# Two small strided reads of the weights at the head of ScalarE's queue, with memsets and filling products in other places

## The chip, the cores and the metric

One core of a Trainium2 chip runs the kernel. The metric is the device time of one execution in microseconds (us), on one core; lower is better. Engines are named as the profile names them: PE (TensorE products), PEld (TensorE weight loads), DVE (VectorE), ACT (ScalarE), POOL (GpSimd), SP (SyncE). SPq and ACTq are the DMA issues of SP and ACT.

## The reference

One transformer block with modulation (adaLN), 2048 tokens of 448 features, bf16:

```python
mod = (_silu(c) @ w_mod).reshape(c.shape[0], 6, 1, -1)
sa, ca, ga, sb, cb, gb = (mod[:, 0].copy(), ..., mod[:, 5].copy())
h = _layernorm(x, axis=-1) * (1 + ca) + sa
x = x + ga * _A_ref(h, A_wqkv, A_wo)
h = _layernorm(x, axis=-1) * (1 + cb) + sb
x = x + gb * _B_ref(h, B_w_in, B_w_sp, B_b_sp, B_w_out)
```

`_A_ref` is attention with 16 heads of 28, in which a token sees itself and the 255 before it. `_B_ref` is a gated MLP: gelu(x @ w_in) is split in two halves of 896, the second is normalised and mixed over all tokens by w_sp (2048 x 2048), multiplied with the first and projected by w_out. w_mod is 448 x 2688, w_qkv 448 x 1344.

## The kernel before

The tokens are 16 tiles of 128; features lie in four chunks of 128 (448 is padded to 512). The program has five streams, one for each engine. The order in each is written out by hand in the table ORDER: a word is the number of an operation in order of definition, the letter of its engine (p, a, v, g, s for PE, ACT, DVE, POOL, SP) and, for some, a slot. Waits on semaphores are derived from the dependencies that each operation names, so each engine works through its list in order, and an operation that waits holds up all behind it.

The stages are: loads, modulation and QKV of tiles 0 to 3 (to some 20 us); attention with the QKV of the other tiles beside it (to some 110 us); the MLP's first product (to some 155 us); mixing over tokens (to some 245 us); projection and output.

The opening, which the change touches, runs so. SP issues the loads one after another: x for tiles 0, 1 (`d_x00`) and 2, 3 (`d_x01`), four chunks of 960 columns of w_mod (`t_wmA`), three chunks of w_qkv's Q and K columns (`t_wq`), the V columns, x for tiles 4 to 7, the rest of w_mod (`t_wmB`), and more. ACT issues c and the last 64 rows of w_qkv (`d_wq3`). DVE clears paddings and takes statistics of x tiles (L580, L583); POOL turns these into rs_all by an addition (L585) and a power (L586); DVE writes the normalised tile xn (L593). TensorE transposes c by products with a one (L520), ACT takes Silu of it into sc_sb (L524, L525), and TensorE multiplies sc_sb with the four chunks of w_mod (L537, one group of eight products for a chunk), which DVE sums into modT (L542). TensorE transposes xn (L624), four tiles in two pairs; each feature chunk is scaled by modT into hT (L634 on ACT, L635 on DVE). Weights for Q and K are spread to 32 columns for a head in WQK (L572, L573), and L644 multiplies WQK and hT: 32 products of 512 columns. Between these stand products of a tile wz of zeros into an unused bank (`warm`, L550), fillers that keep TensorE at work and that nothing reads. L557 is the second use of w_mod, by `t_wmB`; L712 transposes tiles 4 to 7, and L722 scales them into hT. L840 is the exponential of attention.

The fillers' definition, and the group on the fourth w_mod chunk, are

```python
    def warm(n, dur, times, cols):
        for _ in range(n):
            hW = Hold(bH)
            hW.until.append(pe(dur, [lambda e, hW=hW: e.matmul(
```

```python
            [t_wmA[kc], t_sc, t_p2] + t_mA[-1:], -60.0 + 0.1 * kc, [] if kc else [hA]))
```

Of the kernel before, what the change touches and what calls it, by code (L numbers as in the profile page):

```python
# [19 lines left out]
57.v 0.a 3.a 26.v 1.s 2.s 4.s 34.g 23.v 24.v 27.v 43.a 5.s 35.g 6.s 36.g 58.p.0 59.p.0 60.p.0 44.p.0 7.s 139.v 40.g 50.a 32.g 8.s 137.v 37.g 140.v 9.s  # L20
25.v 138.v 143.v 141.g 38.g 10.s 145.v 142.g 146.v 28.v 144.v 45.a 11.s 46.a 147.g 149.v.0 148.g 151.v.1 12.s 61.p.0 62.p.0 63.p.0 64.p.0 65.p.0
66.p.0 67.p.0 68.p.0 69.p.0 70.p.0 150.p.2.3 152.p 13.s 153.v.2 52.p.1 53.p 71.p.0 54.p 155.v.3 14.s 55.p 154.p 29.v 156.p 15.s 16.s 56.v 133.a 157.v
21.s 134.v 158.a 159.v 72.p.0 73.p.0 74.p.0 191.p.4 17.s 171.p.5 135.g 186.p.6 160.v 18.s 161.p.0 136.a 172.p 162.p 192.p 49.g 176.p.1 163.p 47.a
177.p 196.p.2 166.p.3 42.g 193.p 41.g 164.p 213.v 167.p 165.a 173.p 178.p 215.v 168.p 48.a 174.p 51.v 179.p 214.v 217.v 197.p 169.p 175.a 219.v 187.p
198.p 170.a 199.p 39.v 181.p.0 180.a 188.p 218.v 220.v 194.p 216.v 200.v 189.p 221.g 195.a 182.p 222.g 183.p 30.v 184.p 190.a 374.p.0 185.v 205.p.1
375.a.0 229.g 225.g 211.s 227.g 223.g 122.p.0 228.v.0 226.g.1 212.s 201.p.6 224.v.2 19.s 230.g.3 123.v 206.a 380.p.0 125.s 202.v 231.p.0 381.a.1 210.s
234.p.1 232.v 124.s 235.v 399.p.0 233.a 203.p.6 209.s 236.v 400.a.2 269.v 251.p.0 31.v 271.v 401.a 243.p.1 376.v 265.v 126.s 252.a 406.p.0 267.v 127.s
407.a.3 241.p.0 244.v 270.v 266.v 268.v 239.p.1 272.v 204.v 408.a 273.g 274.g 242.v 377.p.0 240.a 402.v 426.p.0 378.v 237.p.0 279.g 427.a.4.0 382.v
277.g 319.v 33.g 428.p.0 281.g 280.v.0 379.p 263.p.1 275.g 320.v 282.v.1 285.s 276.g.2 321.v 238.a 434.p.0 384.v 278.g.3 247.p.0 264.v 435.a.5.1 283.s
409.v 383.p 129.g 249.p.1 248.v 284.s 322.v 411.v 385.p 429.a 455.p.0 131.g 250.v 245.p.0 456.a.6.2 386.v 323.v 286.s 132.g 387.v.0 207.p.1 325.v  # L30
403.p.0 256.s 457.p.0 246.v 208.a 463.p.0 458.a 253.s 404.v 259.p.1 464.a.0.3 438.v 255.s 439.v 405.p 410.p 388.s 261.p.0 430.v 431.v 412.p 262.a
484.p.0 254.s 413.v 287.v 436.p.0 485.a.1.4 414.v.1 257.p.0 459.v 432.p.0 288.v 433.p 290.v 440.p 258.v 437.a 492.p.0 289.v 260.a 465.p.0 489.v 441.p
493.a.2.0 295.p.0 326.v 460.v 442.v 305.p.1 488.v 466.a 324.v 443.v.2 327.g 513.p.0 296.a 328.g 468.v 444.s 515.p.0 514.a.3.1 461.p.0 467.v 462.p
291.p.0 335.g 497.v 415.s 130.g 306.v 469.p 516.a 521.p.0 292.v 329.g 470.p 522.a.4.2 331.g 336.v.0 297.p.1 333.g 332.v.1 330.g.2 471.v 472.v.0
486.p.0 445.p.0 496.v 473.s 487.a 542.p.0 298.a 446.v 494.p.0 543.a.5.3 490.p.0 447.v 22.s 389.p.1 334.v.3 337.s 526.v 491.p 303.p.0 390.v 495.a 517.v
338.s 550.p.0 304.a 525.v 301.p.1 551.a.6.4 546.v 339.s 391.v 293.p.0 518.v 498.p 302.a 340.s 554.v 552.p.0 499.p 294.a 571.p.0 500.v 553.a 501.v.2
474.p.1 310.s 572.a.0.0 307.s 299.p.0 475.v 309.s 476.v 523.p.0 519.p.0 502.s 524.a 555.v 520.p 300.a 579.p.0 448.v 547.v 317.p.1 580.a.1.1 341.g
308.s 477.v 527.p 576.v 528.p 311.p.0 478.g 342.v 479.g 392.v 318.a 529.v 344.v 573.p.0 530.v.1 480.g 600.p.0 574.a 343.g 312.v 416.p.1 531.s
601.a.2.2 449.g 584.v 544.p.0 503.p.0 450.g 417.v 20.s 393.g 575.v 548.p.0 545.a 608.p.0 504.v 549.p 418.v 556.p 609.a.3.3 505.v 315.p.1 419.v 420.g
# [24 lines left out]
1052.a 1051.p 994.g 941.v 1031.v 1072.p.2 1054.a 987.g 880.s 1010.v 898.v 1055.a 915.g 1081.p.3 995.v 1003.v 1011.g 970.v 876.s 1073.p.1 1012.g 959.v
1024.v 1082.p 1004.g 988.v 884.s 1005.g 1013.v 1083.p 1006.v 1074.p 916.v 1086.a 887.s 1075.p 1087.a 1076.a 1100.p.6 1077.a 873.s 1078.a 1079.a 1085.a
# [201 lines left out]
def bass_adaLN_cond__sliding_block__mixer_gmlp__prompt_kernel(  # L267
# [924 lines left out]
```

## Time and profile before

| What | us |
|---|---|
| median of three executions (lowest, highest) | 277.14 (276.2, 277.36) |
| the profiled execution, its whole time | 277.13 |
| its span in the profile | 275.4 |
| PE busy in the span | 265.9 (97%) |
| DVE busy | 162.9 (59%) |
| ACT busy | 128.2 (47%) |
| POOL busy | 111.6 (41%) |

The granted TensorE clock is 1.00 throughout. The page gives the busy share of each engine in 40 slices of 6.9 us, in tenths:

```profile
PE   8898999998999999999999999999999999999995
DVE  7578999997899899696799202110340300341543
ACT  3598899997999999847756500000000000000000
DMA  7995362457344777949699999000000000001123
```

In the stretch from 20 to 110 us, three engines are nearly full; from 155 us on TensorE alone is. A row of the time line has the start, the length from the first instruction's start to the last one's end, engine, line, operation, output and inputs, the number of instructions, and in brackets the idle time of the engine before it with what ended it. A row of the chain of waits has start, length, and what the chain ran through.

### The profile page before, as it was taken

What the parts mean: (1) busy time and instruction counts of PE and PEld (TensorE: products, weight loads), DVE (VectorE), ACT (ScalarE), POOL (GpSimd) and SP (SyncE); (2) the same over time, 40 slices, a digit from 0 to 9 for tenths busy, and PEclk for the clock granted to TensorE, in tenths of its full rate; (3) what the DMA queues carried; (4) which work ended last, traced back from release to release, by engine and by line L of the source; (5) the groups of instructions that cost most, each with busy time, mean ns of one, the idle gap of its engine ahead of it and who ended that gap; (6) DMA issues with size and microseconds to landing.
All of it is one profiled execution on the core that took longest, in us unless ns stands there. A gap on an engine that the chain in (4) does not pass through costs nothing.

```text
span 275.4 us, 7324 instructions
## 1 busy us (share of the span) xinstructions
PE 265.9 (97%) x3174; PEld 139.3 (51%) x3196; DVE 162.9 (59%) x365; ACT 128.2 (47%) x152; POOL 111.6 (41%) x185
## 2 busy tenths in 40 slices
PE   8898999998999999999999999999999999999995
PEld 2544566465667575544444444444444444454452
DVE  7578999997899899696799202110340300341543
ACT  3598899997999999847756500000000000000000
POOL 4440914126644714864549103140361730370400
PEclk9999999999999999999999999999999999999999
DMA  7995362457344777949699999000000000001123
GB/s 207 339 253 147 88 88 33 93 96 204 82 71 71 98 116 153 144 100 167 110 184 175 172 190 187 0 2 0 0 1 2 0 0 0 2 0 33 60 67 109
DMA packets 66862, 26.48 MB, mean 96 GB/s; under 512 B 57801, under 2 KB 65742, under 8 KB 66830
## 3 DMA queue, kind: packets, MB, share of 16 engines
q1 hardware_dynamic: 66748, 25.90, 46.1%
q8 instruction: 25, 0.41, 0.6%
q10 hardware_dynamic: 82, 0.12, 0.1%
q14 instruction: 7, 0.06, 0.1%
HBM read 9.47 MB, written 1.84 MB: 41 GB/s over the span
## 4 chain that ended last, share of the span: by engine, by line
PE 73%; DVE 11%; DMA 7%; ACT 4%; SPq 2%; POOL 1%; issue 1%
PE ps L1077 35%; PE ps L1032 8%; PE ps L1053 8%; PE ps L1094 7%; DMA hT<-o_sb 4%; ACT PW L840 4%; PE ps L947 4%; PE ps L922 3%; PE ps L879 3%; DVE st_all L580 3%; DMA x_sb<-in_A_x_dram 3%; DVE PT L895 2%; PE ps L777 1%; PE ps L764 1%; PE ps L735 1%
## 5 line engine op out<-in xcount | busy, mean ns | idle before, releaser
L840 ACT ACTIVATE PW<-ps 128x2048 bf16<-128x2048 f32 (+1 forms) x56 | 67.1, 1244 | 4.5 <-PE ps L879 1.8
L1081 DVE TENSOR_TENSOR tmpg<-ps,bsp_bc 128x512 bf16<-128x512 f32 x28 | 19.0, 689 | 74.6 <-PE ps L1077 64.6
L1084 POOL TENSOR_TENSOR z1T<-tmpg,z1T 128x512 bf16<-128x512 bf16 x28 | 31.7, 1151 | 73.7 <-DVE tmpg L1081 73.6
L1077 PE MATMUL ps<-wspB,z 128*128 128x512 bf16 x219 | 49.2, 379 | 0.3
L1077 PE MATMUL ps<-wspA,z 128*128 128x512 bf16 x219 | 48.7, 379 | 0.4 <-issue 0.2
L895 DVE TENSOR_TENSOR PT<-PW,mask 128x1024 bf16<-128x1024 bf16 x56 | 36.3, 673 | 0.7 <-ACT PW L840 0.7
L1077 PEld LDWEIGHTS ps<-wspA,z 128*128 128x128 bf16 x224 | 21.8, 98 | 26.6 <-DVE z L1044 0.4
L1077 PEld LDWEIGHTS ps<-wspB,z 128*128 128x128 bf16 x224 | 21.9, 98 | 26.3
L585 POOL TENSOR_SCALAR ve_all<-mv_all 128x1 f32<-128x1 f32 (+2 forms) x37 | 10.1, 280 | 48.3 <-DVE mv_all L583 47.8
L586 POOL TENSOR_TENSOR rs_all<-ve_all,neghalf 128x1 f32<-128x1 f32 (+2 forms) x37 | 26.2, 717 | 1.0
L922 PE MATMUL ps<-Vaug,PT 128*128 128x29 bf16 x496 | 24.8, 176 | 0.0
L922 PEld LDWEIGHTS ps<-Vaug,PT 128*128 128x128 bf16 x496 | 22.3, 96 | 4.4 <-DVE o_sb L938 0.9
L1032 PE MATMUL ps<-w_in,hT 64*128 64x448 bf16 x224 | 22.9, 349 | 0.0
L1053 PE MATMUL ps<-hT,w_in 64*128 64x512 bf16 x196 | 22.5, 376 | 0.0
L1094 PE MATMUL ps<-w_out_g,z1T 128*128 128x448 bf16 x105 | 20.7, 352 | 0.0
L922 PE MATMUL ps<-Vaug,PW 128*128 128x29 bf16 x224 | 20.4, 175 | 0.0
L580 DVE BATCH_NORM_STATS2 st_all<-x_sb 128x6 f32<-128x448 bf16 x32 | 18.9, 613 | 1.5 <-DMA x_sb<-in_A_x_dram 1.4
L580 DVE BATCH_NORM_STATS2 st_all<-z 128x6 f32<-128x448 bf16 x32 | 18.5, 605 | 2.1 <-ACT z L1039 2.0
L735 PE MATMUL ps<-hT,WQK 128*128 128x512 bf16 x69 | 17.8, 380 | 1.4 <-issue 0.3
L922 PEld LDWEIGHTS ps<-Vaug,PW 128*128 128x128 bf16 x224 | 17.7, 96 | 2.2
L1061 ACT ACTIVATE z1T<-ps 128x512 bf16<-128x512 f32 x28 | 14.8, 610 | 7.1 <-PE ps L1053 7.0
L1039 ACT ACTIVATE z<-ps 128x896 bf16<-128x896 f32 x16 | 14.1, 914 | 6.8 <-PE ps L1032 6.8
(112 smaller groups left out, 326.6 us busy)
## 6 DMA issues: line engine op xcount, KB each, us to landing
out_dram<-fin SPq DMA_DIRECT2D x15, 112.0 KB, 1.7
x_sb<-in_A_x_dram SPq DMA_DIRECT2D x3, 448.0 KB, 7.0
w_in<-in_B_w_in_dram SPq DMA_DIRECT2D x1, 1344.0 KB, 6.3
wmod<-in_w_mod_dram SPq DMA_DIRECT2D x1, 1296.0 KB, 10.8
QBD<-qT SPq DMA_DIRECT2D x16, 64.0 KB, 2.9
w_out_g<-in_B_w_out_dram SPq DMA_DIRECT2D x1, 784.0 KB, 5.8
wmod<-in_w_mod_dram SPq DMA_DIRECT2D x3, 240.0 KB, 5.6
wq_st<-in_A_wqkv_dram SPq DMA_DIRECT2D x3, 224.0 KB, 5.8
```

The costliest lines, as they stand in the source:

```text
L580: st = [dve(0.62 if True else 0, lambda e, t=t, ci=ci, s=s: e.bn_stats(st_all[:, slot, t, ci, :], s()), deps(t), prio) for ci, s in enumer ...
L586: rs = pool(0.53 + 0.15 * len(tiles), lambda e: e.tensor_tensor(rs_all[:, slot, a:b], ve_all[:, slot, a:b], neghalf[:, 0:b - a], ALU.pow), ...
L735: m = pe(4 * MMS, [lambda e, h=h, g=g, kc=kc, tb=tb: e.matmul(ps[:, h.slot[0], :], lhsT=WQK[:, kc, 4 * g:4 * g + 4, :].rearrange("p a b -> ...
L840: ex = act(xdur, lambda e, out_ap=out_ap, in_ap=in_ap: e.activation(out_ap(), in_ap(), ACT.Exp, scale=SCALE), [s], v - 8.0 + u, takes, tab ...
L895: return dve(0.70, lambda e: e.tensor_tensor(cols(hp.slot[0] * 2048 + 1024 * k, [[256, 4], [128, 2], [1, 128]]), cols(at_w() + 128 + 192 * ...
L922: fns.append(lambda e, hp=hp, hO=hO, hi=hi, bi=bi, kb=kb, hd=hd, nb=nb, a=at[hi][bi], p_of=p_of: e.matmul(ps[:, hO.slot[0], 32 * hd:32 * h ...
L1032: return lambda e, kc, p0, start, stop: e.matmul(ps[:, hs[t % 2].slot[hf], 0:D], lhsT=hT[p0:p0 + 64, kc, t * 128:(t + 1) * 128], rhs=w_in[ ...
L1053: return lambda e, kc, p0, start, stop: e.matmul(ps[:, hs[b // 2].slot[b % 2], :], lhsT=w_in[p0:p0 + 64, kc, ft * 128:(ft + 1) * 128], rhs ...
L1077: m = pe(16 * MMS, [lambda e, h=h, si=si, ft=ft, tb=tb: e.matmul(ps[:, h.slot[0], :], lhsT=z2[:, si, ft * 128:(ft + 1) * 128], rhs=(wspA i ...
L1081: a = dve(0.7, lambda e, h=h, ht=ht, tb=tb: e.tensor_tensor(tmpg[:, ht.slot[0], :], ps[:, h.slot[0], :], bsp_bc[:, tb * 512:(tb + 1) * 512 ...
L1084: u = pool(1.16, lambda e, ht=ht, ft=ft, tb=tb: e.tensor_tensor(z1T[tb][:, ft, :], tmpg[:, ht.slot[0], :], z1T[tb][:, ft, :], ALU.mult), [ ...
L1094: return [lambda e, ft=ft: e.matmul(ps[:, h.slot[0], 0:D], lhsT=z1T[t // 4][:, ft, (t % 4) * 128:(t % 4 + 1) * 128], rhs=w_out_g[:, ft, :] ...
```

## The change

Six edits, all within the first 10 us of the program:

1. Two loads are added on ACT's queue, into a new tile `early`: 64 rows of w_mod, every seventh, and 32 rows of w_qkv, every fourteenth, 32 columns (64 bytes) of each. The first stands ahead of the load of c, the second between c and `d_wq3`. Nothing reads `early`; the products on the fourth w_mod chunk wait for both loads.
2. On TensorE two fillers move from behind the transposes of c (L520) to ahead of them.
3. On TensorE two more fillers stand between the products on the fourth w_mod chunk and the second pair of transposes.
4. On DVE the memsets of zero, one, sc_sb and sc_sb's single element move ahead of or between the two memsets of wmod.
5. On POOL the first rs_all moves ahead of the memset of WQK's padding.
6. All operation numbers from 4 on rise by two, since two operations are new; this is most of the table's difference.

```diff
+    early, _, _ = alloc("early", [64, 2, 32], BF16)
...
     t_wq3 = load("d_wq3", "act", 0.23, lambda e: e.dma_start(wq_st[0:64, 3, 0:2 * D], A_wqkv[384:448, 0:2 * D]), prio=-98.97, land=5.5)
+    t_early = [load("d_e0", "act", 0.01, lambda e: e.dma_start(early[:, 0, :], w_mod[0:448:7, 0:32]), prio=-98.999, land=3.5),
+               load("d_e1", "act", 0.01, lambda e: e.dma_start(early[0:32, 1, :], A_wqkv[0:448:14, 0:32]), prio=-98.99, land=4.0)]
...
-            [t_wmA[kc], t_sc, t_p2] + t_mA[-1:], -60.0 + 0.1 * kc, [] if kc else [hA]))
+            [t_wmA[kc], t_sc, t_p2] + t_mA[-1:] + (t_early if kc == 3 else []), -60.0 + 0.1 * kc, [] if kc else [hA]))
...
-57.v 0.a 3.a 26.v 1.s 2.s 4.s 34.g 23.v 24.v 27.v 43.a 5.s 35.g 6.s 36.g 58.p.0 59.p.0 60.p.0 44.p.0 7.s 139.v 40.g 50.a 32.g 8.s 137.v 37.g 140.v 9.s
+59.v 4.a 0.a 5.a 3.a 25.v 26.v 27.v 28.v 1.s 2.s 6.s 36.g 30.v 29.v 45.a 7.s 37.g 8.s 38.g 60.p.0 61.p.0 62.p.0 63.p.0 64.p.0 46.p.0 9.s 141.v 42.g
```

The table moves instructions; these are the places. On ACT, the start of its list, before:

```order
L420 DMA c_row<-in_c_dram 1x448
L425 DMA wq_st<-in_A_wqkv_dram 64x896
L518 ACT_TABLE_LOAD
L518 ACTIVATE zero<-zero 128x1 [waits dve]
L529 ACTIVATE QBD<-zero 128x1024
L524 ACTIVATE sc_sb<-ps 128x3 [waits pe,dve]
```

and now (lines are three to seven higher there):

```order
L427 DMA early<-in_w_mod_dram 64x32
L421 DMA c_row<-in_c_dram 1x448
L428 DMA early<-in_A_wqkv_dram 32x32
L426 DMA wq_st<-in_A_wqkv_dram 64x896
L521 ACT_TABLE_LOAD
```

The load of c is second and that of the last w_qkv rows fourth in the queue.

On TensorE, the products on w_mod and the second transposes, before:

```order
L550 MATMUL ps<-wz 128x512
L537 MATMUL ps<-sc_sb,wmod 128x1 [waits d_wmA2]
L537 MATMUL ps<-sc_sb,wmod 128x1 x7
L537 MATMUL ps<-sc_sb,wmod 128x1 [waits d_wmA3]
L537 MATMUL ps<-sc_sb,wmod 128x1 x7
L624 MATMUL ps<-ident,xn 128x128 [waits dve]
```

and now:

```order
L540 MATMUL ps<-sc_sb,wmod 128x1 [waits d_wmA2]
L540 MATMUL ps<-sc_sb,wmod 128x1 x7
L540 MATMUL ps<-sc_sb,wmod 128x1 [waits d_e0,d_e1,d_wmA3]
L540 MATMUL ps<-sc_sb,wmod 128x1 x7
L553 MATMUL ps<-wz 128x512 x2
L627 MATMUL ps<-ident,xn 128x128 [waits dve]
```

Two products of wz stand ahead of the transposes, and the last group waits for the two new loads too.

On POOL, the first statistics, before:

```order
L585 TENSOR_SCALAR ve_all<-mv_all 128x2 [waits dve]
L506 MEMSET WQK 128x128x4
L586 TENSOR_TENSOR rs_all<-ve_all,neghalf 128x2 [waits pool]
L585 TENSOR_SCALAR ve_all<-mv_all 128x2 [waits dve]
L586 TENSOR_TENSOR rs_all<-ve_all,neghalf 128x2 [waits pool]
```

and now:

```order
L588 TENSOR_SCALAR ve_all<-mv_all 128x2 [waits dve]
L589 TENSOR_TENSOR rs_all<-ve_all,neghalf 128x2 [waits pool]
L509 MEMSET WQK 128x128x4
L588 TENSOR_SCALAR ve_all<-mv_all 128x2 [waits dve]
L589 TENSOR_TENSOR rs_all<-ve_all,neghalf 128x2 [waits pool]
```

The memset went from ahead of the first rs_all to behind it.

More of the change, by code (lines that the diff above doesn't have):

```diff
@@ L24 @@
[L24 to L39, printed above, removed]
@@ new lines @@
+249.p.0 266.v 437.a.5.1 285.s 411.v 385.p 131.g 251.p.1 250.v 286.s 324.v 413.v 387.p 431.a 457.p.0 133.g 252.v 247.p.0 458.a.6.2 388.v 325.v 288.s
+134.g 389.v.0 209.p.1 327.v 405.p.0 258.s 459.p.0 248.v 210.a 465.p.0 460.a 255.s 406.v 261.p.1 466.a.0.3 440.v 257.s 441.v 407.p 412.p 390.s 263.p.0
+432.v 433.v 414.p 264.a 486.p.0 256.s 415.v 289.v 438.p.0 487.a.1.4 416.v.1 259.p.0 461.v 434.p.0 290.v 435.p 292.v 442.p 260.v 439.a 494.p.0 291.v
+262.a 467.p.0 491.v 443.p 495.a.2.0 297.p.0 328.v 462.v 444.v 307.p.1 490.v 468.a 326.v 445.v.2 329.g 515.p.0 298.a 330.g 470.v 446.s 517.p.0
@@ new lines @@
+516.a.3.1 463.p.0 469.v 464.p 293.p.0 337.g 499.v 417.s 132.g 308.v 471.p 518.a 523.p.0 294.v 331.g 472.p 524.a.4.2 333.g 338.v.0 299.p.1 335.g
+334.v.1 332.g.2 473.v 474.v.0 488.p.0 447.p.0 498.v 475.s 489.a 544.p.0 300.a 448.v 496.p.0 545.a.5.3 492.p.0 449.v 24.s 391.p.1 336.v.3 339.s 528.v
+493.p 305.p.0 392.v 497.a 519.v 340.s 552.p.0 306.a 527.v 303.p.1 553.a.6.4 548.v 341.s 393.v 295.p.0 520.v 500.p 304.a 342.s 556.v 554.p.0 501.p
+296.a 573.p.0 502.v 555.a 503.v.2 476.p.1 312.s 574.a.0.0 309.s 301.p.0 477.v 311.s 478.v 525.p.0 521.p.0 504.s 526.a 557.v 522.p 302.a 581.p.0 450.v
@@ new lines @@
+456.s 614.v 612.p.0 349.p.0 590.v.2 354.a 644.v 660.p.0 613.a 591.s 608.p.0 350.v 661.a.6.1 563.p.1 615.v 130.s 662.p.0 399.v 643.v 609.p 400.s 616.p
+425.g.0 564.v 663.a 668.p.0 484.v 617.p 664.v 669.a.0.2 315.p.0 357.s 636.v 485.s 633.p.0 565.v 534.p.1 618.v 566.v 316.a 619.v.1 567.g 689.p.0
+512.g.1 634.a 535.v 359.p.0 690.a.1.3 426.g 665.v 427.s 637.p.0 673.v 638.p 641.p.0 360.v 645.p 358.s 642.a 536.v 697.p.0 620.s 646.p 694.v 698.a.2.4
+691.p.0 363.p.1 537.v 647.v 693.v 356.s 538.g 672.v 592.p.0 355.s 364.a 568.g 648.v.0 718.p.0 692.a 513.g 593.v 649.s 569.g 367.p.1 841.g 719.a.3.0
@@ new lines @@
+702.v 666.p.0 670.p.0 514.s 368.v 667.p 674.p 671.a 594.v 726.p.0 723.v 675.p 727.a.4.1 621.p.0 701.v 595.v 699.p.0 596.g 622.v 373.p.1 843.g 866.s
+676.v 700.a 677.v.2 570.g.2 747.p.0 374.v 361.p.0 748.a.5.2 539.g 678.s 623.v 540.g 695.p.0 597.g 722.v 696.p 703.p 598.g 858.s 541.v.0 720.p.0 362.a
+599.g.1 755.p.0 721.a 731.v 704.p 756.a.6.3 650.p.1 542.g 705.v 543.s 706.v.1 749.p.0 365.p.0 651.v 624.v 752.v 750.a 776.p.0 707.s 625.g 751.v
+724.p.0 777.a.0.4 679.p.1 626.g 730.v 627.g 728.p.0 600.v 680.v 725.p 601.s 732.p 759.v 729.a 784.p.0 366.a 571.v 760.v 757.p.0 572.s 733.p 758.a
@@ new lines @@
+928.p 901.a 654.g 655.g 929.p 630.s 656.g 908.p.0 715.g.1 937.a 1034.p.1 685.g 716.v 896.v 770.g 930.a 839.g 717.s 909.p.2 657.v.2 910.p 658.v 938.v
+659.s 795.p.0 686.v.0 912.a 687.g 835.g 824.p.1 796.v 688.s 903.v 911.p 771.g 825.v 944.p.0 772.g 919.a 913.v 836.g 863.s 945.p.3 740.v 914.v 741.g
+773.v.1 946.p 797.v 860.s 947.p 849.v 948.a 774.v 798.v 1042.p.2 850.v 799.g 826.v 857.s 955.a 742.g 950.v 1043.p.0 775.s 743.g 852.g 827.v 931.v
+1044.p 744.v.2 800.g 851.v 1035.p.3 921.v 1047.a 828.g 829.g 1046.a 745.v 957.v 1036.p 746.s 830.g 915.v 902.v 801.g 1037.p 1039.a 831.v.0 1045.p
@@ new lines @@
+832.v 802.v.1 1040.a 833.s 920.v 803.g 962.p.2 1038.a 956.v 1041.a 963.p.1 932.v 1049.a 804.s 1048.a 933.v 964.p 904.v 958.v 895.v 905.g 934.g 980.p.3
+966.a 965.p 871.s 1058.p.0 973.a 981.p.2 853.a 862.s 855.g 974.v 982.p 935.g 1059.p.1 854.g 867.s 984.a 906.g 983.p 986.v 856.g 1060.p 868.s 991.a
+949.v 1061.p 975.v 1063.a 967.v 1066.p.3 865.s 1062.a 993.v 1064.a 1016.p.2 936.v 1065.a 968.v 859.s 1017.p.0 992.v 897.v 1018.p 994.v 976.v 922.v
+985.v 861.s 977.g 1019.p 923.g 978.g 1020.a 998.p.1 898.g 1027.a 1022.v 872.s 1067.p.2 1021.v 951.v 1068.p 1028.v 952.g 864.s 916.g 939.v 899.g
@@ new lines @@
+999.p.0 1071.a 924.g 1023.v 940.v 979.v 1070.a 1069.p 959.g 925.v 870.s 1000.p 995.g 969.v 1029.v 1073.a 970.g 953.g 1001.p 907.v 1002.a 941.g
+1050.p.3 1024.g 942.g 1009.a 1003.v 971.g 1051.p.1 1025.g 1072.a 1010.v 883.s 960.g 1052.p 987.v 1030.v 1011.v 1031.g 988.g 1082.p.0 954.v 1055.a
+1032.g 880.s 1004.v 1054.a 1053.p 996.g 943.v 1033.v 1074.p.2 1056.a 989.g 882.s 1012.v 900.v 1057.a 917.g 1083.p.3 997.v 1005.v 1013.g 972.v 878.s
+1075.p.1 1014.g 961.v 1026.v 1084.p 1006.g 990.v 886.s 1007.g 1015.v 1085.p 1008.v 1076.p 918.v 1088.a 889.s 1077.p 1089.a 1078.a 1102.p.6 1079.a
@@ L75 @@
+1180.p.6 1223.v.0 1227.v.1 1224.s 1228.s 1181.v.3 1182.s
 """
```

63 lines of the change are left out of this document (25 added, 38 removed).

## The prediction

> **What bounds the kernel now.** I read the chain of waits first, then the time line of the first 25 us, then the DMA rates in stretches. The change touches nothing after 10 us, so the question is what an opening that is earlier or later is worth. The chain, in order of time, start and length in us:
>
> ```profile
> 6.51 7.00 DMA x_sb<-in_A_x_dram
> 13.53 1.15 DVE st_all L580 x2
> 21.43 0.62 PE ps L712 x8
> 22.08 1.01 DVE hT L722 x2
> ```
>
> The end hangs on token tiles 4 to 7: load, statistics, normalised copy, TensorE transposes (L712), copy into hT (L722). Behind that VectorE has no gap for 20 us (the view by stretches: length, busy time of PE, PEld, DVE, ACT and POOL, granted TensorE clock, DMA share, GB/s):
>
> ```profile
> 25.00:45.00 20.00, 19.22 (x420) 10.96 (x422) 20.00 (x52) 18.88 (x20) 8.14 (x14) 1.00 0.37 72
> 2.75:3.75 1.00, 0.96 (x6) 0.57 (x7) 0.83 (x2) 0.99 (x3) 0.00 (x0) 1.00 1.27 377
> 3.75:5.25 1.50, 1.50 (x5) 0.52 (x4) 1.50 (x6) 0.58 (x1) 0.07 (x1) 1.00 0.76 206
> 5.25:6.50 1.25, 1.25 (x5) 0.43 (x4) 1.13 (x5) 0.00 (x1) 1.25 (x3) 1.00 1.04 370
> 6.50:8.50 2.00, 2.00 (x28) 1.21 (x26) 1.39 (x5) 0.22 (x2) 1.12 (x3) 1.00 1.06 253
> ```
>
> VectorE is busy 20.00 of 20.00 us there, so whatever L722 gains or loses is passed on whole. The loads run at 377 GB/s, drop to 206 as w_mod is first read (x and the part of w_qkv on ScalarE's queue are through by 3.75), recover, and drop to 253 as the main part of w_qkv begins. Against a mean of 373 the first drop loses 1.5 x (1 - 206/373) = 0.67 us, the second, against 370, 2.0 x (1 - 253/370) = 0.63 us; together 1.30 us. The TensorE clock is 1.00 in all rows. Who waits for these loads:
>
> ```profile
> 7.17 0.61 PE L624 MATMUL ps<-ident,xn 128*128 128x128 bf16 x8
> 7.62 0.67 PE L537 MATMUL ps<-sc_sb,wmod 128*128 128x1 bf16 x16
> 8.15 0.38 PE L550 MATMUL ps<-wz 128*128 128x512 bf16 x1
> 8.73 0.35 PE L537 MATMUL ps<-sc_sb,wmod 128*128 128x1 bf16 x8 [0.21 <-DMA wmod<-in_w_mod_dram]
> 9.37 0.35 PE L537 MATMUL ps<-sc_sb,wmod 128*128 128x1 bf16 x8 [0.29 <-DMA wmod<-in_w_mod_dram]
> 9.59 0.61 PE L624 MATMUL ps<-ident,xn 128*128 128x128 bf16 x8
> 10.03 0.81 PE L550 MATMUL ps<-wz 128*128 128x512 bf16 x3
> 9.72 0.95 ACT L572 ACTIVATE WQK<-wq_st 128x896 bf16<-128x896 bf16 x1 [3.00 <-DMA wq_st<-in_A_wqkv_dram]
> 10.23 0.54 DVE L635 TENSOR_SCALAR hT<-ps,modT 128x512 bf16<-128x512 bf16 x1 [0.28 <-PE ps L624]
> 11.06 6.85 PE L644 MATMUL ps<-hT,WQK 128*128 128x512 bf16 x31 [0.22 <-DVE hT L635]
> ```
>
> TensorE works in order. The fourth chunk of w_mod lets it go on at 9.37; the second transposes follow at 9.59, the first hT at 10.23, the first QK projection at 11.06, and 31 of its 32 products then run without a gap. The first WQK also waits for a load, until 9.72.
>
> **The change part by part.** *The two touches on ScalarE's queue.* They carry 96 x 64 bytes, about 6 KB: 0.02 us at 373 GB/s. Their issues come before the load of c and between it and wq3. These rows price them:
>
> ```profile
> 0.79 0.51 ACTq L420 DMA_DIRECT2D c_row<-in_c_dram  x1
> 1.34 0.52 ACTq L425 DMA_DIRECT2D wq_st<-in_A_wqkv_dram  x1
> 3.29 1.04 ACT L529 ACTIVATE QBD<-zero 128x1024 f32<-128x1024 f32 x1
> 6.50 0.18 ACT L524 ACTIVATE sc_sb<-ps 128x3 bf16<-128x3 f32 x1 [2.17 <-DVE sc_sb L495]
> 2.79 0.35 PE L520 MATMUL ps<-one,c_row 1*128 1x1 bf16 x4 [0.29 <-DVE one L492]
> ```
>
> Two issues of 0.55 us each (1.34 - 0.79) put ScalarE's table load, Silu and QBD clearing 1.1 us later: the clearing ends at 5.4 instead of 4.33. ScalarE then waited 2.17 us until 6.50 for a memset, so this is covered, and costs at most 0.1 were the cover gone. c is issued 0.55 later; two of the ten fillers now stand ahead of its products (L520, 2.79) and give them until about 3.6. sc_sb is first used at 7.62. Nothing here is on the path.
>
> What the touches give: if the drops come from first contact with each region, they are paid while x is loaded. The lower bound is no gain; the upper one is both drops, 1.30 us. The fourth w_mod chunk lies wholly behind the first drop: by 6.50 about 206 x 1.5 + 370 x 1.25 = 772 KB of the 860 KB in the four chunks (448 rows of 960 bf16) have moved, and its tail runs in the second. I take 0.7 to 1.0 us, nearer the first drop: it lands at 8.4 to 8.7. The first w_qkv chunk then comes about as much earlier than 9.72, and tiles 4 to 7 up to 1.30 earlier than 13.53.
>
> By the Trainium skill (HBM Reference, Latency) an access costs 0.2 us on average and 2 us under high load, with no word of first contact; by it the drops belong to load, a touch cures nothing, and the sum is that of the second rival below. No run here separates the two yet; the recovery to 370 between the drops, at full load, speaks against it.
>
> *Two fillers between the last w_mod products and the second transposes.* The three at 10.03 take 0.81 and one 0.38, so one costs (0.81 - 0.38)/2 = 0.215 us, two 0.43. They are in order, so the transposes start at (landing + 0.22 + 0.43) instead of landing + 0.22. The touch must bring the landing at least 0.43 earlier to break even.
>
> *Moved memsets and the POOL swap.*
>
> ```profile
> 1.32 1.18 DVE L493 MEMSET wmod<- 64x1344 uint32 x1 [0.34 <-issue]
> 3.72 1.15 DVE L580 BATCH_NORM_STATS2 st_all<-x_sb 128x6 f32<-128x448 bf16 x2
> 5.18 0.23 POOL L585 TENSOR_SCALAR ve_all<-mv_all 128x2 f32<-128x2 f32 x1 [2.91 <-DVE mv_all L583]
> 5.35 0.53 POOL L506 MEMSET WQK<- 128x512 bf16 x1
> 5.84 0.73 POOL L586 TENSOR_TENSOR rs_all<-ve_all,neghalf 128x2 f32<-128x2 f32 x1
> 6.50 0.18 DVE L583 BATCH_NORM_AGGREGATE mv_all<-st_all 128x2 f32<-128x6 f32 x1
> 6.62 0.70 DVE L593 TENSOR_SCALAR xn<-x_sb,mv_all,rs_all 128x448 bf16<-128x448 bf16 x2
> 7.93 0.70 DVE L593 TENSOR_SCALAR xn<-x_sb,mv_all,rs_all 128x448 bf16<-128x448 bf16 x2 [0.61 <-POOL rs_all L586]
> ```
>
> The tiny memsets go ahead of the 1.18 us one, into its 0.34 us of idle, so the statistics still start near 3.7 (bounds -0.1 to +0.2). The first rs_all no longer queues behind the 0.53 us memset and starts about 0.35 earlier; but the last aggregation at 6.50 stands ahead of xn on VectorE and loses only a memset, so xn comes about 0.15 earlier, 6.47. The second pair, 7.93, gains under 0.1: the WQK memset now stands ahead of its ve_all. It is needed at 9.59, so this is covered by over 0.9 us.
>
> *The sum at the first hT.* With nothing to wait for, TensorE would do: first transposes at 7.0, sixteen products at 7.45 to 8.0, a filler, two groups of 0.22, two fillers of 0.215, and the second transposes near 9.1. That floor caps the gain at about 0.45. With the landing at 8.4 to 8.7 they start at 9.1 to 9.35: 0.24 to 0.45 earlier; I take 0.35, and 11.06 becomes 10.7.
>
> *From there to L722.*
>
> ```profile
> 7.73 0.53 SPq L409 DMA_DIRECT2D wmod<-in_w_mod_dram  x1
> wmod<-in_w_mod_dram SPq DMA_DIRECT2D x1, 216.0 KB, 11.3
> 19.13 0.53 PEld L557 LDWEIGHTS ps<-wmod,sc_rep 128*32 128x32 bf16 x16 [0.58 <-DVE qT L653]
> 20.90 0.12 PEld L853 LDWEIGHTS ps<-qT,KT 32*128 32x128 bf16 x8 [0.37 <-ACT PT L840]
> 21.43 1.05 PE L712 MATMUL ps<-ident,xn 128*128 128x128 bf16 x16 [0.24 <-POOL xn L599]
> ```
>
> The L557 products wait for the last part of w_mod (7.73 + 11.3 = 19.03, though the row names VectorE), and the transposes at 21.43 wait 0.24 for xn of tiles 4 to 7. Both come up to 1.30 earlier with the loads. But L853 in between waits for ScalarE's exponentials, which follow the QK block and so move by 0.35 alone. At L712 the gain is 0.35 + 0.24 = 0.59 us, at least 0.35.
>
> The profiled execution has a span of 275.4 us and took 277.13, so 1.73 lie around the span; the median is 277.14, the same for this purpose. 277.13 - 0.59 = **276.5 us**, its own range 276.0 to 277.0.
>
> **The rivals.** *More than the opening.* The chain also holds waits on transposing DMAs whose start depends on the order of arrival:
>
> ```profile
> 45.10 4.12 DMA hT<-o_sb
> 60.47 4.20 DMA hT<-o_sb
> ```
>
> ```profile
> hT<-o_sb SPq DMA_TRANSPOSE x16, 3.4
> ```
>
> The list of DMA issues gives 3.4 us as the median of this group, so 0.7 to 0.8 of each could go if transfers meet less traffic: 276.5 - 1.5 = 275.0 to, with one, 275.7. For it: they are on the chain. Against it: nothing in the change reaches them but the shift.
>
> *The touches change nothing.* If the drops are traffic and not first contact, the landing stays at 9.37 and the fillers stand naked: +0.43 at 11.06, all passed on: 277.6. For it: the second drop comes although w_qkv was already read in part by wq3.
>
> *The touches hold up x* (slower). 64 and 32 rows, spread evenly over 16 DMA engines, are four and two packets on each, ahead of or among the x tiles. If each first contact blocks its engine, x arrives late, the statistics move from 3.72, and the second xn (7.93, its first tile done at 8.3) comes later by as much. With the transposes at 9.2 the cover is 0.9 us; from there it decides. One stall per region, 0.67 + 0.63 = 1.30 us, would leave the transposes where they are now (8.3 + 1.3 - 0.1 = 9.5 against 9.59); six in a row, 4 x 0.67 + 2 x 0.63 = 3.9 us, put them at 12.1, 2.5 late, 279.6. Stalls of one engine may overlap in part; I take 3.0 us, +1.6, 278.7. Against it: x itself, also at first contact, ran at 377 GB/s at once. The rule that speaks for it is in the Trainium skill, DMA: Bandwidth & Descriptors, section Issuing engines are not separate DMA queues: transfers from any engine share the same 16 DMA engines and interleave, so ScalarE's queue is no side road. No row here shows the touch's own time.
>
> **How the numbers follow.** Forecast 0.46, more than the opening 0.27, nothing changed 0.12, x held up 0.15. A measurement of this kernel cannot tell less than 0.5%, 1.39 us, from no change: bounds 275.75 and 278.53. Faster takes the 0.27 and 0.07 of the forecast's lower tail: 0.34. Slower: 0.15 and 0.03 from the second rival with a larger stall: 0.18. Same: 0.48. The range reaches from within the first rival to short of the last: 275.0 to 278.2.
>
> **What would show it.** In the profile after: rates in 3.75 to 5.25 and 6.5 to 8.5 near 370 if the touch works, 206 and 253 if not; the fourth w_mod wait (now until 9.37) at 8.4 to 8.7, two fillers behind it, the second transposes at 9.1 to 9.35; the first L644 near 10.7, L712 near 20.8. If the first statistics start after 4.5, x was held up. Wrong it would be if the L644 block moves by more than 0.5 us either way, or if its shift isn't the shift of the end.

## The result, and the profile after

The change takes 278.84 us in the median of 20 executions (276.59 to 281.96), the kernel before 277.12 beside it; the ratio is 1.0053, with an interval of 1.0029 to 1.0078. It is slower by 0.5%: 0.0053 of 277.12 is 1.5 us. (The ratio leaves out the change's three longest executions, which ran at a lower clock; the medians, 1.72 apart, count them.) The profiled execution took 279.0 us with a span of 277.3, so 1.9 us more than the one profiled before. Lines lie three higher from here on (L540 is L537, L627 is L624, L638 is L635, L647 is L644, L715 is L712).

The time line of the opening:

```profile
0.80 0.55 ACTq L427 DMA_DIRECT2D early<-in_w_mod_dram  x1
2.09 0.34 ACTq L428 DMA_DIRECT2D early<-in_A_wqkv_dram  x1
3.65 1.16 DVE L583 BATCH_NORM_STATS2 st_all<-x_sb 128x6 f32<-128x448 bf16 x2
6.26 0.81 DVE L596 TENSOR_SCALAR xn<-x_sb,mv_all,rs_all 128x448 bf16<-128x448 bf16 x2
9.66 0.35 PE L540 MATMUL ps<-sc_sb,wmod 128*128 128x1 bf16 x8 [0.22 <-DMA wmod<-in_w_mod_dram]
9.88 0.59 PE L553 MATMUL ps<-wz 128*128 128x512 bf16 x2
10.31 0.61 PE L627 MATMUL ps<-ident,xn 128*128 128x128 bf16 x8
10.96 0.54 DVE L638 TENSOR_SCALAR hT<-ps,modT 128x512 bf16<-128x512 bf16 x1 [0.71 <-PE ps L627]
11.42 0.39 DVE L576 COPY WQK<-wq_st 128x896 bf16<-128x896 bf16 x1
11.53 1.05 POOL L576 COPY WQK<-wq_st 128x896 bf16<-128x896 bf16 x1 [3.88 <-DMA wq_st<-in_A_wqkv_dram]
11.79 6.85 PE L647 MATMUL ps<-hT,WQK 128*128 128x512 bf16 x31 [0.22 <-DVE hT L638]
21.80 1.05 PE L715 MATMUL ps<-ident,xn 128*128 128x128 bf16 x16
```

The fourth w_mod chunk lets TensorE go on at 9.66 and not at 9.37, 0.29 later. The second transposes start 0.65 behind it where they started 0.22 behind it: the two fillers cost 0.43. So L647 starts 0.73 later. (One of the 32 products has no record in either trace; the first, by its distance from hT.) The statistics start at 3.65, against 3.72: x was not held up. The list of DMA issues has 2.8 us to landing for the touch of w_mod (the first small read) and 4.3 for that of w_qkv, so they landed at 3.6 and 6.4, and the wait for them at the fourth w_mod chunk costs nothing of its own:

```profile
early<-in_w_mod_dram ACTq DMA_DIRECT2D x1, 4.0 KB, 2.8
early<-in_A_wqkv_dram ACTq DMA_DIRECT2D x1, 2.0 KB, 4.3
```

The load rates (the view by stretches, columns as before):

```profile
2.75:3.75 1.00, 0.81 (x6) 0.20 (x4) 0.90 (x2) 0.78 (x1) 0.00 (x0) 1.00 1.01 289
3.75:5.25 1.50, 1.50 (x8) 0.68 (x7) 1.50 (x5) 1.49 (x3) 0.14 (x1) 1.00 0.92 228
5.25:6.50 1.25, 0.97 (x5) 0.23 (x3) 1.22 (x5) 0.28 (x3) 1.17 (x3) 1.00 0.90 307
6.50:8.50 2.00, 1.21 (x22) 0.89 (x23) 1.27 (x4) 0.00 (x0) 1.06 (x3) 1.00 1.05 274
```

In this profile the drop at w_mod is still there, 228 GB/s against 206, and the stretches beside it are slower: 289 against 377, 307 against 370. The chain of waits, start and length:

```profile
3.26 6.36 DMA wmod<-in_w_mod_dram
11.79 6.85 PE ps L647 x31
86.52 4.25 DMA hT<-o_sb
90.81 0.93 PE ps L950 x4
```

It now begins with w_mod's load and runs through L647. At L715 the lateness is down to 0.37 (21.80 against 21.43), and near 90 us it grows to 2.1 at once. There TensorE waits for a transposing DMA that it did not wait for before. SP's queue in that place, after and then before:

```profile
79.63 6.20 SPq L484 DMA_TRANSPOSE hT<-xn  x2
85.87 0.60 SPq L681 DMA_DIRECT2D QBD<-qT  x1
86.52 1.26 SPq L484 DMA_TRANSPOSE hT<-o_sb  x1
```

```profile
78.88 5.02 SPq L481 DMA_TRANSPOSE hT<-xn  x2
83.94 1.34 SPq L678 DMA_DIRECT2D QBD<-qT  x1
85.33 1.27 SPq L481 DMA_TRANSPOSE hT<-o_sb  x1
```

The two transposes of xn hold the queue until 85.83 instead of 83.90, so the next of o_sb is issued 1.19 later and lands at 86.52 + 4.25 = 90.77, where L950 starts. This does not belong to every execution of the change: of the twenty profiles of this document, TensorE waits 1.3 to 1.4 us at this place in this one, in the change's second (e13) and in that of e1, which has no touches; in the change's third (e18) it does not. In these three the two transposes of xn take 5.80 to 6.20 us, in the other seventeen 3.60 to 5.33.

### The profile page after: what moved, and what is told of

The parts are those of the page before. It is cut to its first block, busy times and chain, and to the rows that moved or that the text cites. A ratio compares the mean times of both kernels' runs of the same rounds, so it can differ in the third digit from the quotient of the medians.

```text
span 277.3 us, 7331 instructions
## 1 busy us (share of the span) xinstructions
PE 265.8 (96%) x3176; PEld 139.2 (50%) x3198; DVE 163.6 (59%) x365; ACT 128.2 (46%) x152; POOL 112.5 (41%) x185
## 4 chain that ended last, share of the span: by engine, by line
PE 67%; DVE 14%; DMA 7%; POOL 5%; ACT 4%; issue 1%; SPq 1%
PE ps L1080 35%; PE ps L1097 7%; PE ps L1035 7%; DMA hT<-o_sb 5%; DVE PT L898 5%; ACT PW L843 4%; PE ps L1056 4%; POOL rs_all L589 3%; PE ps L950 3%; DVE st_all L583 3%; PE ps L647 2%; DMA wmod<-in_w_mod_dram 2%; PE ps L925 2%; PE ps L882 2%; PE ps L738 1%
## 5 line engine op out<-in xcount | busy, mean ns | idle before, releaser
L588 POOL TENSOR_SCALAR ve_all<-mv_all 128x1 f32<-128x1 f32 (+2 forms) x37 | 11.0, 304 | 49.1 <-DVE mv_all L586 48.6
```

## The experiments

In the table ORDER, with the change's numbers, 4 and 5 are the two small reads ("touches") of w_mod and w_qkv, 0 is the load of c, 3 is wq3, 77 and 78 the added fillers, 63 and 64 the moved ones, 136.v VectorE's copy of the second w_qkv chunk into WQK, and 137.g GpSimd's copy of the third. All ratios are to the kernel before, run beside each.

### One part left out, or one alone

The change without touches; without the two added fillers; the kernel before with only the moves of memsets and rs_all; the kernel before with only the touches:

```diff
 e1_no_touch, from the change
-59.v 4.a 0.a 5.a 3.a
+59.v 0.a 3.a
-+ t_mA[-1:] + (t_early if kc == 3 else [])
++ t_mA[-1:]
 e2_no_fill, from the change
-57.p 77.p.0 78.p.0 156.p
+57.p 156.p
 e4_moves_only, from e1_no_touch: also without 77.p.0 78.p.0, and 63.p.0 64.p.0 back behind 46.p.0
 e5_touch_only, from the kernel before
+4.a ahead of 0.a, 5.a ahead of 3.a, and the wait for both at kc == 3
```

> The change without the two touches; all else of it stays (fillers, memsets, POOL order). Theory 'fillers and a late landing, added up': the landing of the fourth w_mod chunk returns to about 9.37, the fillers still cost 0.43, so the first QK product starts at 11.4 to 11.5 and the time is 277.4 to 278.0, ratio to before 1.001 to 1.003. Rival 'the touches do the harm' (late loads beyond the opening): the time is that of before or less, ratio 0.998 to 1.000, whatever the fillers do.

> The change without the two fillers between the last w_mod products and the second transposes. Theory 'added up': the landing stays at 9.6, the first QK product starts at 11.35 instead of 11.79, 277.6 to 278.2, ratio 1.002 to 1.004. Rival 'the touches do the harm': as the change, ratio about 1.005. Rival 'the fillers do the harm': ratio 1.000.

> Before with the moved memsets and the POOL order alone, no touches, no added or moved fillers. All theories: the first xn about 0.3 earlier, but the fourth w_mod landing unchanged near 9.4, so the first QK product within 0.1 of 11.06 and the time within 0.3 us of before, ratio 0.999 to 1.001. If it is slower by 0.003 or more, the moves are part of the cause.

> Before with the two touches and the wait for them alone. Theory 'added up': the fourth w_mod landing near 9.6, c later so that TensorE idles 0.7 us before the transposed c, the first QK product at 11.3, ratio 1.001 to 1.003. Rival 'the touches do the harm': ratio 1.004 to 1.006. If touches did bring the landing forward, 8.4 to 8.7 and a ratio under 1.000.

Measured: without touches 1.0016 (0.9995 to 1.0038), without fillers 1.0038 (1.0014 to 1.0062), moves alone 1.0004 (0.9985 to 1.0024), touches alone 1.0059 (1.0032 to 1.0086). The moves cost nothing that can be measured; the touches do.

### How the touches cost: behind the loads, and one load late

If they push wq3 onto w_mod's load, they do no harm behind wq3, and wq3 alone, issued late, does:

```diff
 e6_behind, from the change
-4.a 0.a 5.a 3.a
+0.a 3.a 4.a 5.a
 e7_wq3_late, from the kernel before (45.a is the table load with Silu)
-0.a 3.a ... 45.a
+0.a ... 45.a 3.a
```

> The change with its two touches behind wq3 on ScalarE's queue (c, wq3, touch, touch) instead of around c. Theory 'wq3 pushed onto w_mod' (the touches cost by moving the 112 KB of wq3, which ran beside x, into the stretch of the w_mod chunks, 0.3 us of the rate): wq3 lands near 4.6 again, the touches cost nothing, ratio as without touches, 1.000 to 1.002. Rival 'the touches themselves hold up the DMA engines': the stalls come, now beside w_mod, ratio 1.003 to 1.006.

> Before, without any touch, with the issue of wq3 moved behind the table load and first Silu of ScalarE, so that it starts at about 2.9 instead of 1.34. Theory 'wq3 pushed onto w_mod': the w_mod landing 0.3 later, ratio 1.002 to 1.004. Rival 'the touches themselves': 0.999 to 1.001.

Behind wq3: 1.0054 (1.0025 to 1.0084); wq3 late: 1.0013 (0.9984 to 1.0041). The idea falls: wq3 landed at 7.6 in e7 and cost nothing that can be measured, and behind wq3 the touches cost as much as ahead of it.

### Which touch

```diff
 e8_wmod_touch and e9_wqkv_touch: e4_moves_only with one of them
+4.a ahead of 0.a, or 5.a ahead of 3.a
 e10_no_wqkv_touch, from the change
-4.a 0.a 5.a 3.a
+4.a 0.a 3.a
 e12_other_matrix, from the change; e11_alone_other the same in e9_wqkv_touch
-early[0:32, 1, :], A_wqkv[0:448:14, 0:32]
+early[0:32, 1, :], w_mod[0:448:14, 0:32]
```

Where one touch is left out, the products on the fourth w_mod chunk wait for the other alone.

> The moved memsets and POOL order (which alone gave 1.0004) with the touch of w_mod alone, ahead of c; no fillers added or moved. Theory 'wq3 pushed': wq3 0.55 later, ratio 1.001 to 1.002. Rival 'the touches themselves': the w_mod touch has 64 of the 96 rows, two thirds of the harm, 1.002 to 1.004. Were the touch of use, the drop of the rate at w_mod is gone and the ratio under 1.000.

> As the last, with the touch of w_qkv alone, between c and wq3. Theory 'wq3 pushed': wq3 0.5 later, ratio 1.001 to 1.002. Rival 'the touches themselves': one third of the harm, 1.001.

> The whole change without the transfer that reads w_qkv: the one on w_mod, the two fillers, the moves of memsets and POOL stay. Theory R (the w_qkv transfer is what costs): ratio 1.001 to 1.002 (the fillers' 0.0012 and nothing else). Theory S (either small transfer costs, about half each): 1.003 or more, like the whole change less 0.0017. Mean clocks of 0.993 in none or one execution by R, in several by S.

> The whole change, but the second small transfer reads every fourteenth row of w_mod instead of w_qkv; number, size, place and queue of the transfers as in the change. Theory R (it is the matrix that is read): ratio near 1.0012 to 1.002. Theory S (it is the second transfer itself, whatever it reads: its time in the queues): 1.005, as the change.

> The kernel before with the memset moves and the POOL swap and one small transfer in the place of the second one (between the loads of c and wq3), reading 32 rows of w_mod instead of w_qkv. The same with w_qkv gave 1.0026. Theory R: 1.0005, as with the w_mod transfer ahead of c. Theory S (place between c and wq3, 32 rows): 1.0026.

> The change itself once more, on the same chip as the three others: 1.005 in the mean of its executions by every theory; its profile tells how far the landing of the fourth part of w_mod (9.66 us in the first profile) and the shift behind 88 us (+2.1 us) repeat. If the landing is scatter between executions, it comes out anywhere between 8.6 and 10.1; if it is the change's, again near 9.7.

Alone, w_mod's touch gave 1.0005 (0.9985 to 1.0025), w_qkv's 1.0026 (0.9997 to 1.0054). That looked like w_qkv, and is not: without it the change is at 1.0063 (1.0032 to 1.0095), with the other matrix at 1.0068 (1.0042 to 1.0094), and the other matrix alone at 1.0038 (1.0011 to 1.0065). The change itself, beside them, gave 1.0064 (1.0024 to 1.0104). Theory R, that the w_qkv touch is what costs, falls. In the change's second profile the first QK product starts at 11.40, and the copy on ScalarE that waits for the first w_qkv chunk at 9.87, against 11.79 and 10.06 in its first profile and 11.06 and 9.72 in the kernel before.

The profiles of these kernels show something else, on VectorE and GpSimd. The time line of the change's second profile:

```profile
10.80 0.54 DVE L638 TENSOR_SCALAR hT<-ps,modT 128x512 bf16<-128x512 bf16 x1 [0.71 <-PE ps L627]
11.18 0.93 POOL L576 COPY WQK<-wq_st 128x896 bf16<-128x896 bf16 x1 [3.53 <-DMA wq_st<-in_A_wqkv_dram]
11.27 1.98 DVE L576 COPY WQK<-wq_st 128x896 bf16<-128x896 bf16 x1
11.40 1.04 PE L647 MATMUL ps<-hT,WQK 128*128 128x512 bf16 x4
12.04 0.95 POOL L533 MEMSET QBD<- 128x1024 f32 x1
13.39 6.20 PE L647 MATMUL ps<-hT,WQK 128*128 128x512 bf16 x28 [0.95 <-DVE WQK L576]
```

and the same place in the kernel before:

```profile
10.69 0.38 DVE L573 COPY WQK<-wq_st 128x896 bf16<-128x896 bf16 x1
11.10 0.93 POOL L573 COPY WQK<-wq_st 128x896 bf16<-128x896 bf16 x1 [3.21 <-DMA wq_st<-in_A_wqkv_dram]
11.97 0.95 POOL L530 MEMSET QBD<- 128x1024 f32 x1
```

VectorE's copy takes 0.38 or 0.39 us if it starts before GpSimd's. If GpSimd's is first, here by 0.09 (in e10 by 0.04), it takes 1.98: it ends at 13.25, 0.26 behind the end of GpSimd's next instruction, the memset (12.04 + 0.95 = 12.99), so it stood still for both. TensorE does four products and then waits 0.95 for it. In this profile the copy lies on the chain of waits:

```profile
11.35 1.91 DVE WQK L576
13.39 6.20 PE ps L647 x28
```

The profile of the w_mod touch alone shows the same with one instruction less: VectorE starts when only the memset is left, and ends at 12.33, again 0.26 behind it:

```profile
3.70 4.45 PE L553 MATMUL ps<-wz 128*128 128x512 bf16 x10
7.95 1.06 PE L627 MATMUL ps<-ident,xn 128*128 128x128 bf16 x8
10.52 0.81 PE L553 MATMUL ps<-wz 128*128 128x512 bf16 x3
11.12 0.95 POOL L533 MEMSET QBD<- 128x1024 f32 x1
11.19 1.14 DVE L576 COPY WQK<-wq_st 128x896 bf16<-128x896 bf16 x1
```

That kernel has no fillers between, and its loads were early. TensorE made it late: ten products of wz take 4.45 us there, (4.45 - 0.63)/9 = 0.42 for each behind the first, which is 0.63 long, where the three at 10.52 have (0.81 - 0.38)/2 = 0.22, and the transposes take 1.06 instead of 0.61. (The view by stretches gives its clock as 1.00 there; the lengths of the products tell more.)

By the Trainium skill (SBUF — State Buffer, section SBUF: two separate sides) a VectorE operation in a two-port mode and a GpSimd one share a port pair under an exclusive lock: who starts first keeps it for the whole instruction, the other stands. For VectorE the trace agrees, and shows that the waiting copy does not get in between two GpSimd instructions either; that this copy runs in such a mode no run shows. GpSimd's copy, when it is second, stands for less than the whole: it takes 1.05 in the change's first profile and 1.15 in e3, 0.12 and 0.22 more than its 0.93. In e6 the profile has it first by 0.01 us, and yet it is the longer one (1.18); at such a distance the starts do not tell the order.

In the kernel before, VectorE's copy has 0.41 us in hand (11.10 - 10.69). It hangs on hT, and so on the fillers; GpSimd's hangs on its load alone. Two fillers take 0.43 of those 0.41.

### Taking the collision away

```diff
 e14_dve_both and e17_before_both, from the change and from the kernel before
-137.g
+137.v behind 161.v, the second hT
 e16_held and e19_held_again, from the change, in the dependencies of the copies
+[t_wqk[1]] if kc == 2
 e3_fill_only, from the kernel before
+77.p.0 78.p.0 behind 57.p
 e18_third: the change
```

> The whole change, with GpSimd's copy of the third w_qkv chunk into WQK put on VectorE, behind its own copy and the next hT. Theory P (the two copies collide on the way to the on-chip memory): both VectorE copies take 0.38 us, the QK products run without a gap behind the fourth, and the ratio to the kernel before falls from 1.0053 to 1.0064 to 1.002 or less (what the bare fillers cost, 0.43 us, and the touches' landing). Theory T (the touches' traffic is what costs): ratio stays at 1.005 or above, since loads and touches are the same.

> The whole change, with GpSimd's copy of the third chunk made to wait until VectorE's copy of the second is done; nothing else is moved. Theory P: VectorE's copy 0.38 us in the profile, GpSimd's starts just behind it, ratio 1.002 to 1.003. Theory T: 1.005 or above.

> The kernel before with only the two added fillers between the last w_mod products and the second transposes. Theory P: VectorE's copy starts about 0.43 us later and meets GpSimd's in part of the executions; a gap of 0.9 to 1.0 us in the QK products where it does; ratio 1.002 to 1.005 and wider spread than the kernel before. Theory T: 0.43 us at most, ratio 1.0016 or less, copy 0.38 us.

> The kernel before with GpSimd's copy of the third w_qkv chunk put on VectorE; no touches, fillers or moves. Theory P: the kernel before has 0.41 us between the two copies and rarely collides, so 0.998 to 1.000, with a narrower spread. Theory T: 1.000.

> The change itself, beside the held version on the same chip. Theory P: 1.005 as in its two other batches, with the held version at least 0.0025 lower; in the profile either VectorE's copy takes 1.95 to 2.03 us and the first QK block has a gap near 0.95 us, or GpSimd's copy starts within 0.1 us behind it. Theory T: the held version the same as this within 0.001.

> The held version again (GpSimd's copy of the third chunk waits for VectorE's of the second), beside the change. Theory P: 1.000 to 1.0025 to the kernel before, copy 0.38 us, no gap. Theory T: as the change, 1.005.

Both copies on VectorE: 1.0039 (1.0001 to 1.0077). GpSimd's held: 1.0003 (0.9969 to 1.0037). Fillers alone: 0.9992 (0.9963 to 1.0021). The kernel before with both on VectorE: 1.0001 (0.9967 to 1.0036). Then, side by side, the change 1.0055 (1.0020 to 1.0091) and the held version 1.0054 (1.0026 to 1.0082). In the profiles the collision is gone as expected (copy 0.38, no gap). In the times its price is not shown: one of the two held runs met theory P (the collision is what costs) and the other theory T (the touches' traffic is), and the one comparison side by side, 1.0055 with 1.0054, shows no difference. No version is faster than the kernel before beyond the noise.

All profiles together, from their time lines (copy of WQK on VectorE, start of GpSimd's copy, which waits for the load of the third w_qkv chunk, end of the last L647, all in us):

| kernel | ratio | GpSimd's start | VectorE's start, length | QK's end | profiled execution |
|---|---|---|---|---|---|
| before | 1 | 11.10 | 10.69, 0.38 | 17.91 | 277.13 |
| e4 moves alone | 1.0004 | 10.78 | 10.18, 0.38 | 17.40 | 276.42 |
| e7 wq3 late | 1.0013 | 10.69 | 10.26, 0.39 | 17.59 | 276.48 |
| e17 before, both on VectorE | 1.0001 | - | 10.73, 0.38 | 17.95 | 277.04 |
| e3 fillers | 0.9992 | 10.89 | 10.87, 0.39 | 18.08 | 277.95 |
| e1 fillers, moves | 1.0016 | 10.16 | 10.27, **1.95** | 18.57 | 280.23 |
| e2 touches, moves | 1.0038 | 10.76 | 10.37, 0.38 | 17.64 | 276.52 |
| e5 touches | 1.0059 | 11.72 | 11.37, 0.39 | 18.59 | 278.44 |
| e8 w_mod touch | 1.0005 | 10.25 | 11.19, **1.14** | 18.67 | 277.53 |
| e9 w_qkv touch | 1.0026 | 10.68 | 10.24, 0.38 | 17.49 | 277.82 |
| e11 other matrix alone | 1.0038 | 10.91 | 10.55, 0.39 | 17.77 | 277.43 |
| the change | 1.0053 | 11.53 | 11.42, 0.39 | 18.64 | 279.00 |
| e13 the change | 1.0064 | 11.18 | 11.27, **1.98** | 19.59 | 279.23 |
| e18 the change | 1.0055 | 11.12 | 11.23, **1.95** | 19.53 | 279.33 |
| e6 touches behind | 1.0054 | 10.57 | 10.58, 0.38 | 17.80 | 279.71 |
| e10 without w_qkv's | 1.0063 | 10.96 | 11.00, **2.03** | 19.37 | 278.04 |
| e12 other matrix | 1.0068 | 11.09 | 11.18, **1.97** | 19.50 | 279.08 |
| e14 both on VectorE | 1.0039 | - | 11.12, 0.38 | 18.34 | 277.14 |
| e16 held | 1.0003 | 12.01 | 11.56, 0.38 | 18.78 | 277.92 |
| e19 held | 1.0054 | 11.89 | 11.44, 0.38 | 18.66 | 277.44 |

Three readings. First, GpSimd's start tells when the third w_qkv chunk has landed: without touches it lies between 10.16 and 11.10 (mean 10.72 of five), with them between 10.25 and 11.72 (mean 10.98 of eleven; the two held ones wait for VectorE). ScalarE's first copy into WQK, which waits for the first w_qkv chunk, starts at 8.85 to 9.76 in the six without (mean 9.42) and at 8.99 to 10.40 in the fourteen with (mean 9.74). Touches do not bring loads forward. That they delay them by 0.3 us is likely but not sure, since single profiles of either kind lie 0.9 to 1.4 apart; and e6 is at 1.0054 although this copy starts at 9.23 there. The rate from 3.75 to 5.25 us says more: 206 to 320 GB/s in the six without touches (mean 258), 168 to 269 in the fourteen with them (mean 210). Second, with the fillers and GpSimd's copy left free, VectorE's copy is held up in five of eight profiles, and starts within 0.12 us of GpSimd's in the other three; without the fillers it is held up in one of eight (e8). Third, a later end of QK goes with a later end of the program: over 18 of the 20 (without e1, profiled in an execution 3.2 us above its kernel's median, and e6, whose clock fell) a straight line has a slope of 1.05 and leaves 0.5 us. These kernels differ in touches too, so the line alone does not show the cause.

By groups: touches with fillers, six measurements, 1.0053 to 1.0068; touches with the fillers out or the copies kept apart, eight, mean 1.0033 (1.0003 to 1.0059); fillers without touches, two, mean 1.0004; neither, three, mean 1.0006.

## Why the prediction was wrong

The forecast was 276.5 us in a range of 275.0 to 278.2; the change takes 278.6 by its ratio, beyond the range and the other way.

*What bounds the kernel*: right in that the opening is on the path, but not in the branch. The prediction has the end hang on x of tiles 4 to 7; the change's chain begins with w_mod's load and runs through L647. Of the 0.73 at L647 only 0.37 is left at L715, where the kernel before had waited 0.24 for xn of these tiles. "Passed on whole" failed in this profile: 0.37 at L715 became 1.9 at the end, most of it in the wait near 90 us.

*What the touches give*: this step failed: "if the drops come from first contact with each region, they are paid while x is loaded", with a landing at 8.4 to 8.7. It was measured at 9.66, and the first w_qkv chunk, forecast about as much earlier than 9.72, let ScalarE go on at 10.06; with the landing 0.29 later and not 0.7 to 1.0 earlier, the two fillers' 0.43 stood uncovered. Nor is the drop at w_mod a constant of the region: the touch of w_mod was issued 2.95 us ahead of that stretch and landed before it, and the rate there is 228 GB/s; without any touch it is 206 in the kernel before, the lowest of six, and up to 320. So the 0.67 us that the touch was to save was read from one execution, at the low end of what such loads do. The prediction also has wq3 through by 3.75; its issue is at 1.34 and the list of DMA issues of the kernel before gives 3.3 us to landing, so it landed at 4.6, and the stretch holds its end too:

```profile
wq_st<-in_A_wqkv_dram ACTq DMA_DIRECT2D x1, 112.0 KB, 3.3
```

The recovery between the drops, which I held against load as their cause, was too weak a sign. The rule that I set against it, of the Trainium skill (HBM Reference, Latency), by which a touch cures nothing, agrees with these landings in that nothing came earlier. What makes the drops is not shown.

*The two fillers*: right to the hundredth, 0.43 from the landing to the transposes. So was the break-even, which the touches missed. This is the second rival, "the touches change nothing", in its mechanism: fillers naked, +0.43. It fell short in size, 277.6, since it too let nothing else happen.

*Moved memsets and the POOL swap*: right in the sign and in costing nothing; xn starts at 6.26 against 6.62 (0.36 earlier, 0.15 was forecast), and alone the moves measure 1.0004.

*x held up*: its time, 278.7, was near the measured one by luck: its mechanism is refuted, with the statistics at 3.65.

*From there to L722*: what was missing here is the price of the QK block itself, 32 products "without a gap". I asked of every moved engine only whether its own result was needed later. I did not ask what VectorE's copy would meet on its way when it came 0.43 later. The copies appear in no part of the prediction: VectorE's with 0.41 us in hand against 0.43 of fillers. The collision is shown by the traces, and its price at QK's end: the 32 products take 8.19 us in the change's second profile (11.40 to 19.59), and 7.08 in the second held one (11.58 to 18.66), so 1.1 us. The first profile, 279.00 us long, has no such gap, so the collision is not what made that one late. How much of the 0.5% it makes is not settled: with it taken away, 1.0039, 1.0003 and 1.0054.

As an estimate from these runs: 0.43 for the fillers, 0.3 for the later landing, 1.1 times two of three for the collision, and up to 0.5 for the clock (below) make 1.9 us, with 1.5 to 1.8 measured. That the sum comes out does not prove its parts. Without touches the landing and the clock fall away, and the fillers with the collision should leave 0.43 + 0.73 = 1.2 us, a ratio of 1.0042; the two measurements of that, 1.0016 (up to 1.0038) and 0.9992 (up to 1.0021), are below it. So the parts do not simply add up, or the collision is rarer there. What is shown is that the touches cost time and save none; how they cost it is open.

Open are why the two transposes of xn near 80 us hold SP's queue for 5.80 to 6.20 us in three profiles and less in the others, and why the load rate is lower with touches that carry 6 KB.

## What to carry to other kernels

A product that only fills time still moves what waits behind it in order. Before placing one, list each operation that it delays, and for each ask not only who needs its result but which engine it will now run beside: VectorE behind GpSimd here paid 1.6 us for being 0.1 late. Where two such copies lie 0.4 us apart, their order is a margin like any other, and is written down or forced. A dip in the rate of loads is no proof of a cost that can be paid early: first see whether it repeats in place and size: here five other kernels without touches have 240 to 320 GB/s where the kernel before has 206.

## What the hardware showed besides

*A stretch at a lower clock.* The profile of e6 has it, near the end of attention (the view by stretches; the clock is the third figure from the right):

```profile
105.00:110.00 5.00, 3.00 (x35) 1.44 (x34) 4.97 (x13) 2.26 (x4) 3.95 (x6) 0.87 0.66 184
110.00:115.00 5.00, 5.00 (x78) 2.78 (x76) 0.94 (x4) 4.40 (x6) 0.71 (x2) 0.79 0.68 123
```

5 x 0.13 + 5 x 0.21 = 1.7 us of clock are missing; in stretches of 1 us the clock reads 0.50 from 109 to 112 us, so this is 3.4 us at half speed. TensorE has 2.00 us without work just before, up to 108.20. The Trainium skill (TensorE: Matmul & The Clock Gate, What's actually happening) has the clock halve after an idle window of some 3.4 us; here it halves 0.5 us behind an idle stretch of 2.00 us, which is shorter than that, and stays at half for about one such window. Of the executions whose clock is listed, 40 of 159 with touches have a mean clock below 0.997 (0.988 to 0.994), and 15 of 206 without. In the change's first 20 such executions (7) take 280.35 us in the mean, the others 278.19. With a frequency 0.18 higher and 2.2 us each, that is 0.4 us, and 0.5 for the change itself (12 of 38). That the touches cause it is not shown beyond this count, and no run shows how they could.

*Small transfers are slow beside the loads.* The 32 rows of 64 bytes, 2 KB, landed 2.3 us after issue in e9 and 4.3 us in the change and in e5; in none of the profiles sooner than 2.3.

*The same loads vary.* In the stretch from 3.75 to 5.25 us, 206 GB/s before became 251 with the moves alone and 263 with both copies on VectorE (e17), both without any touch.
